# Extra rows of w4 on five DMA engines, wide value products on four column groups, and a new order of the tail

## The chip, the cores and the metric

The kernel runs on one core of one Trainium2 chip. Its engines are named PE (matmul; PEld is its weight load), DVE (vector), ACT (scalar), POOL (GpSimd) and SP, which here only issues DMAs. The metric is the device time in microseconds of one execution; the median over several is used. The profile's span runs from the first to the last instruction of the program, so an execution's time is somewhat longer than its span.

## The reference

One token (B = S = 1, D = 512) passes a layer norm; an attention over the last 4096 of 32768 cached positions, with 32 heads of 128, is multiplied by a gate that comes from a small MLP, and the input is added:

```python
def reference(...):
    x = A_x
    xn = _layernorm(x)
    s = _A_ref(xn, A_k_cache, A_v_cache, A_wq, A_wo)   # attention, below
    g = _silu(_B_ref(xn, B_w1, B_w2, B_w3, B_w4))
    return x + s * g

# _A_ref, W = 4096, Dh = 128, 32 heads
q = (xn @ wq) per head
scores = einsum("bhqd,bhkd->bhqk", q, k_cache[:, :, -W:]) * Dh ** -0.5
o = einsum("bhqk,bhkd->bhqd", softmax(scores), v_cache[:, :, -W:])
return o.reshape(1, 1, 4096) @ wo

# _B_ref, S = 1: the shifts by one and two positions leave only zeros of h
x1 = xn + shifted @ w2                                  # shifted is all zeros
return x1 + _gelu(_layernorm(x1) @ w3) @ w4             # w3 512x1376, w4 1376x512
```

All inputs and the output are bf16. Keys and values of the window are 32 MB each; with the weights 78.84 MB are read from HBM.

## The kernel before, in words

Everything is loaded through SP's queue, by one helper `load` (L79), in program order: w2, w3, w4, wq, then keys and values. A transfer that needs a buffer which is still in use holds up SP, and all transfers behind it.

**Start.** x is normalised; the MLP runs as a chain of small steps on PE, ACT, DVE and POOL: `a_ps` (L217, the product with w3, whose columns are split into ten chunks of 128 and one of 96), gelu into `a_bf`, `hr_ps` (L225, L228: rows of w2 and w4 as moving operand, 512 wide, one matmul for each chunk), the gate `g_row`. Then q: `qT_ps` (L244) and its broadcast `q_bc`. The tiles of tag "misc" share one PSUM buffer, so each of these steps waits for the one before it to be read out. Outside the region described next, a scheduler places the instructions on their engines.

**Groups.** The 32 heads are taken in 8 groups of 4 (`G`). A group's keys are one 4 MB transfer (`load_kv`), its values another. A tile `kv` has 128 partitions and `CP` = 128 columns of 128 elements. The keys' scores are formed in two ways: columns 0 to `nd(g)` - 1 (64 to 80) on DVE (`k_vector`: product L308, sum L310, four parts), the others on PE (`k_turn`: transposes L324, copied out by ACT L326; `k_scores` L332). The softmax of a group is cut into `sm_own`, `sm_max`, `sm_turn` (L354, L356, L358), `sm_exp` (L363 to L370), `sm_den` (L376) and `sm_rden` (L381).

**Values.** `v_part` multiplies the values by the probabilities `pT`. Ordinary groups use 128 matmuls with a weight load of 128x128 values and 4 moving columns (L430). The groups in `MOVED` use 32 matmuls that load 16 columns of `pT` and move four columns of values, 512 wide (L422), into `ov`; ACT copies it (L425), and `v_add` (L437), in the next step, adds the four wanted blocks. `v_out` scales by the softmax's denominator into `o_blk`.

**Order.** In `tc.manual_schedule` the program's order on PE, DVE and ACT is the order written. Step s handles the keys of group s and the values of group h = s - 2. There are three buffers for keys (one of them is later used for a part of wo) and two for values, so the values of group 7 can be loaded only when those of group 5 have been used, which is the last PE work of step 7. Steps 8 and 9 are the tail: the last softmax, the values of groups 6 and 7, the latter in three pieces (`cuts`, columns 64, 112, 128).

**Output.** o times wo is taken in blocks of heads: 16 heads in a 512 wide product (`y_wide`), 8 (`y_block(1)`) and the last 8. A block's o is first redistributed over the partitions: `ox_spread` (DVE), `ox_pick` (a matmul L468, then DVE L470 and L474). The product is `rows_add` (L150): four matmuls of 128 columns, each with a weight of one column, into four rows 32 partitions apart of `y_ps`. Of the last 8 heads, the first 320 rows of wo (`wo_few`, two loads of 160 KB, with 5 as the outer dimension of their access pattern) go through `ox_few`, the rest head by head (`y_head`, `wo_rows`). `few` and `perm` are permutation matrices made from the identity.

The lines that the text speaks of stand below.

Of the kernel before, what the change touches and what calls it, by code (L numbers as in the profile page):

```python
# [24 lines left out]
LATE = 7  # L25
MOVED = (0, 2)


@with_exitstack
def kernel(  # L30
# [27 lines left out]
    F = B_w3.shape[1]  # L58
    assert F == 10 * P + 96
    scale = float(Dh) ** -0.5  # L60
# [28 lines left out]
    load(w3_sb[:], B_w3.rearrange("(p c) n -> p c n", p=P))  # L89
    w4_sb = wts.tile([P, 11, D], BF16, name="w4_sb")  # L90
    load(w4_sb[:, 0:10, :], B_w4[0:10 * P, :].rearrange("(p c) n -> p c n", p=P))
    load(w4_sb[0:96, 10, :], B_w4[10 * P:F, :])
    wq_sb = wts.tile([P, KC, HD], BF16, name="wq_sb")

    load(wq_sb[:].rearrange("p c n -> p (c n)"), A_wq.rearrange("(a b c) n -> b a (c n)", a=2, c=KC))

# [78 lines left out]


    x_f = small.tile([P, KC], FP32, name="x_f")
    nc.vector.tensor_copy(out=x_f[:], in_=x_bf[:])
# [6 lines left out]

    perm = wts.tile([P, P // 2, 2], BF16, name="perm")
    nc.vector.tensor_copy(out=perm[:], in_=ident_bf[:].rearrange("k (a b) -> k b a", a=2))
    xq_ps = ps_tr.tile([P, KC], FP32, tag="pt", name="xq_ps")
# [22 lines left out]

    chunks = [(P, slice(r, 10 * P, 10)) for r in range(10)]
    chunks += [(96, slice(10 * P, F, 1))]
    a_ps = ps_misc.tile([P, 11], FP32, tag="misc", name="a_ps")
    for j, (m, cols) in enumerate(chunks):
        for c in range(KC):
            nc.tensor.matmul(a_ps[0:m, j:j + 1], lhsT=w3_sb[:, c, cols], rhs=z3_bf[:, c:c + 1],  # L217
                             start=(c == 0), stop=(c == KC - 1))
    a_bf = small.tile([P, 11], BF16, name="a_bf")
    nc.scalar.activation(out=a_bf[:, 0:10], in_=a_ps[:, 0:10], func=ACT.Gelu_apprx_tanh)  # L220
    nc.scalar.activation(out=a_bf[0:96, 10:11], in_=a_ps[0:96, 10:11], func=ACT.Gelu_apprx_tanh)

    hr_ps = ps_misc.tile([1, D], FP32, tag="misc", name="hr_ps")
    for c in range(KC):
        nc.tensor.matmul(hr_ps[:], lhsT=shifted_bf[:, c:c + 1], rhs=w2_sb[:, c, :], start=(c == 0),  # L225
                         stop=False)
    for i, (m, _) in enumerate(chunks):
        nc.tensor.matmul(hr_ps[:], lhsT=a_bf[0:m, i:i + 1], rhs=w4_sb[0:m, i, :], start=False,  # L228
                         stop=(i == len(chunks) - 1))
# [30 lines left out]
    make_masks(8)  # L260

    few = const.tile([P, 2, 32], BF16, name="few")
    nc.vector.memset(few[:], 0.0)
    for c in range(2):
        nc.vector.tensor_copy(
            out=few[:, c, 0:4 * NE].rearrange("p (a b) -> p a b", b=4),
            in_=ident_bf[:, 4 * NE * c:4 * NE * (c + 1)].rearrange("p (b a) -> p a b", b=4))

# [16 lines left out]
    nc.vector.tensor_scalar(out=md[:], in0=ident_f[0:1 + G, 1:1 + G], scalar1=-1.0, scalar2=1e30,  # L289
                            op0=ALU.add, op1=ALU.mult)  # L290

    st = {}
# [91 lines left out]

    blocks = [(0, 16), (16, 8), (24, 8)]
    few_block = 2
    few_h = blocks[few_block][0]
    FEW = 8 * 8 * NE
    h_part = few_h + FEW // P

    r_part = FEW % P
    o_blk, wo_blk, ox_blk = {}, {}, {}
# [4 lines left out]

    def load_few():
        t = wo_blk[few_block]
        for c in range(2):  # L400
            r0 = few_h * P + c * FEW // 2
            load(t[32 * c:32 * c + 4 * NE],
                 A_wo[r0:r0 + FEW // 2, :].rearrange("(b a t) n -> a b (t n)", b=4, a=NE))

    def wo_row(h):
        return wo_rows[:, h - h_part, :]

    def load_rows(h, n):
        if h == h_part:
            load(wo_rows[r_part:P, 0, :], A_wo[h * P + r_part:(h + 1) * P, :])  # L410
            h, n = h + 1, n - 1
        load(wo_rows[:, h - h_part:h - h_part + n, :],
             A_wo[h * P:(h + n) * P, :].rearrange("(h p) n -> p h n", p=P))
# [3 lines left out]
    def v_part(g, v, c0=0, c1=CP):  # L417
        s = st[g]
        if g in MOVED:
            s["ov"] = ps_o.tile([4 * G, 4, Dh], FP32, tag="oT", name="ov")  # L420
            for c in range(0, CP, 4):
                nc.tensor.matmul(s["ov"][:], lhsT=s["pT"][:, c:c + 4, :].rearrange("p i a -> p (i a)"),  # L422
                                 rhs=v[:, c:c + 4, :], start=(c == 0), stop=(c == CP - 4))
            s["ov_sb"] = sm_pool.tile([4 * G, 4, Dh], FP32, tag="ov_sb", bufs=1, name="ov_sb")
            nc.scalar.copy(out=s["ov_sb"][:], in_=s["ov"][:])  # L425
            return
        if c0 == 0:
            s["oT"] = ps_o.tile([P, G], FP32, tag="oT", name="oT")
        for c in range(c0, c1):
            nc.tensor.matmul(s["oT"][:], lhsT=v[:, c, :], rhs=s["pT"][:, c, :], start=(c == 0),  # L430
                             stop=(c == CP - 1))

    def v_add(g):
        s = st[g]
        s["oT"] = ps_misc.tile([P, G], FP32, tag="misc", name="oT")
        for j in range(4):
            nc.tensor.matmul(s["oT"][:], lhsT=s["ov_sb"][:, j, :], rhs=ident_f[0:4 * G, G * j:G * j + G],  # L437
                             start=(j == 0), stop=(j == 3))

    def v_out(g):  # L440
        h = G * g
        b = [i for i, (h0, _) in enumerate(blocks) if h >= h0][-1]
        if b not in o_blk:
            o_blk[b] = sm_pool.tile([P, blocks[b][1]], BF16, tag=f"o{b}", bufs=1, name="o")
            if b == few_block:
                nc.gpsimd.memset(o_blk[b][:], 0.0)
        c = h - blocks[b][0]
        if g >= NG - 2:
            nc.vector.tensor_tensor(out=o_blk[b][:, c:c + G], in0=st[g]["oT"][:], in1=st[g]["rden"][:],  # L449
                                    op=ALU.mult)  # L450
            return
        for k in range(G):
            nc.scalar.mul(o_blk[b][:, c + k:c + k + 1], st[g]["oT"][:, k:k + 1], st[g]["rden"][:, k:k + 1])  # L453
# [23 lines left out]

    def ox_few(i):
        of_ps = ps_misc.tile([64, 8], FP32, tag="misc", name="of_ps")
        nc.tensor.matmul(of_ps[:], lhsT=few[:].rearrange("p a b -> p (a b)"), rhs=ox_blk[i][:],  # L480
                         start=True, stop=True)
        of = sm_pool.tile([64, 8], BF16, tag="of", bufs=1, name="of")
        nc.vector.tensor_copy(out=of[:], in_=of_ps[:])
        ox_blk[i] = of


    y_row = small.tile([1, D], FP32, name="y_row")
# [13 lines left out]
    def y_block(i):  # L501
        for t in range(8):
            rows_add(y_ps, ox_blk[i][:, t:t + 1], wo_blk[i][:, t, :], False)

    def y_head(h):
        rows_add(y_ps, o_blk[few_block][:, h - few_h:h - few_h + 1], wo_row(h), h == H - 1)

# [6 lines left out]
    for s in range(NG + LAG):  # L514
# [3 lines left out]
        if s == LAG:  # L518
            wts_guard.__exit__(None, None, None)
            v_pool = ctx.enter_context(tc.tile_pool(name="v", bufs=V_BUFS))  # L520
            wo_blk[few_block] = v_pool.tile([64, 8, D], BF16, tag="wo_few", bufs=1, name="wo_few")
            nc.gpsimd.memset(wo_blk[few_block][:], 0.0)
            wo_rows = v_pool.tile([P, H - h_part, D], BF16, tag="wo_rows", bufs=1, name="wo_rows")
            nc.gpsimd.memset(wo_rows[0:r_part, 0, :], 0.0)
        if last:
            load_rows(h_part, 2)
            v = load_kv(v_pool, A_v_cache, h, cuts)
            for r, n in ((H - G, 2), (H - 2, 1), (H - 1, 1)):
                load_rows(r, n)
        elif h >= 0:  # L530
            v = load_kv(v_pool, A_v_cache, h)
# [4 lines left out]
        if h == 5:  # L536
            load_wo(1)
            load_few()

# [40 lines left out]
        elif s == NG:  # L580

            sm_den(NG - 2)
            sm_rden(NG - 2)
            sm_turn(NG - 1)
            ox_spread(1)
            sm_exp(NG - 1)
            ox_pick(1)
            y_block(1)
            rows_add(y_ps, one_f, y_row, False)
            v_part(h, v)  # L590
            v_out(h)
            ox_spread(few_block)
            sm_den(NG - 1)
            sm_rden(NG - 1)
            ox_pick(few_block)
            ox_few(few_block)
        else:
            v_part(h, v, 0, cuts[1])
            y_block(few_block)
            for r in range(h_part, H - G):  # L600
                y_head(r)
            for c0, c1 in zip(cuts[1:], cuts[2:]):
                v_part(h, v, c0, c1)
            v_out(h)
            for r in range(H - G, H):
                y_head(r)
# [36 lines left out]
```

## Time and profile before

| what | value |
| --- | --- |
| times of four runs | 194.95, 195.37, 195.49, 196.83 us; median 195.43 |
| the profiled execution | 195.49 us, span 193.6 us |
| instructions | 4769, of them PE 2123 matmuls with as many weight loads |
| PE, PEld, DVE, ACT, POOL busy | 136.2, 103.0, 143.7, 87.2, 6.4 us |
| HBM read | 78.84 MB, 407 GB/s over the span |
| mean granted TensorE clock | 0.667 of full |

Busy time of an engine counts only instructions that compute. A row of the timeline gives start and length in us, engine, line, operation, what it writes and reads, shapes, how many were joined, and in brackets how long the engine stood idle before and what released it; "issue" means that the profile shows nothing it waited for. A row of the chain gives start, length, and what the time went to. The rows of digits cut the span into 40 slices of 4.84 us.

### The profile page before, as it was taken

To read this page: it belongs to the slowest core of one execution; us is meant where nothing else is said; L and a number is where in the kernel's file an instruction comes from. 1 tells how busy PE (TensorE), PEld (TensorE's weight loads), DVE (VectorE), ACT (ScalarE), POOL (GpSimd) and SP (SyncE) were. 2 spreads that over 40 slices of the span, in tenths; PEclk is the share of its full clock that TensorE was granted. 3 is DMA by queue.
4 is the path that set the end of the run, shared out by engine and by line. 5 is a ranking of instruction groups with operands and counts; after the bars stand their busy time and mean duration, and the time that the engine had idled before them with its cause. 6 is when DMAs were issued, how large, how long until landed. Compare 5 with 4: busy or idle time off the path is not lost.

```text
span 193.6 us, 4769 instructions
## 1 busy us (share of the span) xinstructions
PE 136.2 (70%) x2123; PEld 103.0 (53%) x2123; DVE 143.7 (74%) x162; ACT 87.2 (45%) x195; POOL 6.4 (3%) x14
## 2 busy tenths in 40 slices
PE   0559774987726589888898978820978968835782
PEld 0454363866625533567784348720868357824761
DVE  1550108999999999999999999980999999931201
ACT  2003003888896350498567056810574088723000
POOL 2110008000000000000000000000000000000000
PEclk9999955575765557996555798555555696755555
DMA  5999899999999999999999999999999999999970
GB/s 202 424 498 433 372 416 425 406 433 430 433 430 433 433 435 430 433 433 430 433 430 433 430 433 416 450 430 430 433 433 425 433 430 405 459 431 371 417 294 1
DMA packets 4725, 79.13 MB, mean 409 GB/s; under 512 B 666, under 2 KB 1466, under 8 KB 1722
## 3 DMA queue, kind: packets, MB, share of 16 engines
q1 hardware_dynamic: 4554, 78.84, 95.7%
q8 instruction: 16, 0.26, 0.5%
q10 hardware_dynamic: 152, 0.00, 0.0%
q14 instruction: 3, 0.02, 0.0%
HBM read 78.84 MB, written 0.00 MB: 407 GB/s over the span
## 4 chain that ended last, share of the span: by engine, by line
DVE 43%; DMA 31%; PE 18%; issue 4%; ACT 3%; POOL 1%; POOLq 0%; ACTq 0%; SPq 0%
DVE S L310 25%; DMA kv<-in_A_v_cache_dram 15%; DMA kv<-in_A_k_cache_dram 14%; DVE prod L308 14%; PE oT L430 6%; DMA x_bf<-in_A_x_dram 2%; PE hr_ps L228 2%; PE pt L324 2%; PE qT_ps L244 2%; ACT kt L326 2%; PE a_ps L217 1%; PE y_ps L150 1%; PE hr_ps L225 1%; PE sT L332 1%; DVE S L346 1%
## 5 line engine op out<-in xcount | busy, mean ns | idle before, releaser
L310 DVE TENSOR_REDUCE S<-prod 128x20 f32<-128x2560 bf16 (+2 forms) x32 | 82.2, 2570 | 1.1
L326 ACT COPY kt<-pt 128x1024 bf16<-128x1024 bf16 (+1 forms) x56 | 54.7, 1008 | 21.3 <-PE pt L324 20.6
L324 PE MATMUL pt<-ident_bf,kv 128*128 128x128 bf16 x444 | 46.5, 274 | 8.5 <-DMA kv<-in_A_k_cache_dram 8.5
L308 DVE TENSOR_TENSOR prod<-kv,q_bc 128x2560 bf16<-128x2560 bf16 (+2 forms) x32 | 43.5, 1361 | 8.0 <-DMA kv<-in_A_k_cache_dram 5.6
L324 PEld LDWEIGHTS <-kv 128*128 128x128 bf16 x444 | 37.5, 126 | 10.5 <-DMA kv<-in_A_k_cache_dram 8.9
L332 PE MATMUL sT<-qT_bf,kt 128*128 128x4 bf16 x444 | 20.7, 168 | 17.1 <-ACT kt L326 16.2
L332 PEld LDWEIGHTS <-kt 128*128 128x128 bf16 x444 | 17.1, 104 | 24.6 <-ACT kt L326 24.2
L430 PE MATMUL oT<-pT,kv 128*128 128x4 bf16 x768 | 22.1, 166 | 6.8 <-issue 5.4
L430 PEld LDWEIGHTS <-kv 128*128 128x128 bf16 x768 | 21.4, 104 | 8.8 <-issue 6.1
L422 PE MATMUL ov<-kv,pT 128*16 128x512 bf16 x64 | 19.9, 486 | 0.0
L370 ACT ACTIVATE pT<-S,mb 128x128 bf16<-128x128 f32 x32 | 13.9, 570 | 0.3
L422 PEld LDWEIGHTS <-pT 128*16 128x16 bf16 x64 | 6.8, 109 | 12.1 <-issue 8.0
L449 DVE TENSOR_TENSOR o<-oT,rden 128x4 bf16<-128x4 f32 x2 | 0.3, 162 | 12.7 <-PE oT L430 12.7
L453 ACT ACTIVATE o<-oT,rden 128x1 bf16<-128x1 f32 x24 | 4.3, 260 | 11.8 <-PE oT L430 9.2
L341 ACT ACTIVATE own<-sT,par 128x48 f32<-128x48 f32 (+2 forms) x32 | 7.6, 361 | 3.7 <-PE sT L332 3.7
L425 ACT COPY ov_sb<-ov 16x512 f32<-16x512 f32 x2 | 1.1, 575 | 15.6 <-PE ov L422 15.6
L370 ACT ACTIVATION_READ_ACCUMULATOR pT<-S,mb 128x1 f32 x32 | 8.2, 255 | 0.0
L231 DVE COPY hr<-hr_ps 1x512 f32<-1x512 f32 x1 | 0.7, 679 | 8.6 <-PE hr_ps L228 8.6
L496 PE MATMUL yr_ps<-wo,ox 128*1 128x512 bf16 x16 | 5.2, 494 | 0.9 <-DVE ox L474 0.9
L220 ACT ACTIVATE a_bf<-a_ps 128x10 bf16<-128x10 f32 x1 | 0.2, 179 | 11.9 <-PE a_ps L217 11.9
L363 PE MATMUL mb_ps<-md,par_t 5*128 5x4 f32 x16 | 4.2, 329 | 1.7 <-DVE md L358 1.0
L363 PEld LDWEIGHTS mb_ps<-md,par_t 5*128 5x128 f32 x16 | 3.6, 276 | 2.1 <-PE sT L332 1.1
(117 smaller groups left out, 90.3 us busy)
## 6 DMA issues: line engine op xcount, KB each, us to landing
kv<-in_A_k_cache_dram SPq DMA_DIRECT2D x7, 4096.0 KB, 29.7
kv<-in_A_v_cache_dram SPq DMA_DIRECT2D x7, 4096.0 KB, 33.3
wq_sb<-in_A_wq_dram SPq DMA_DIRECT2D x1, 4096.0 KB, 18.2
kv<-in_A_k_cache_dram SPq DMA_DIRECT2D x2, 2048.0 KB, 22.5
wo<-in_A_wo_dram SPq DMA_DIRECT2D x1, 2048.0 KB
kv<-in_A_v_cache_dram SPq DMA_DIRECT2D x1, 2048.0 KB, 11.5
kv<-in_A_v_cache_dram SPq DMA_DIRECT2D x1, 1536.0 KB, 14.6
w_sb<-in_B_w_dram SPq DMA_DIRECT2D x1, 1376.0 KB
```

The source lines that it names most:

```text
L308: nc.vector.tensor_tensor(out=prod[:, 0:m, :], in0=kn[:, rows, :], in1=q_bc[:, g:g + 1, :].to_broadcast([P, m, Dh]), op=ALU.mult)
L310: nc.vector.tensor_reduce(out=st[g]["S"][:, rows], in_=prod[:, 0:m, :], axis=AX.X, op=ALU.add)
L324: nc.tensor.transpose(pt[:, c - c0, :], kn[:, c, :], ident_bf[:])
L326: nc.scalar.copy(out=kts[b][:, 0:c1 - c0, :], in_=pt[:, 0:c1 - c0, :])
L332: nc.tensor.matmul(st[g]["sT"][:, c - nd(g), :], lhsT=kt[:, c - c0, :], rhs=qT_bf[:, G * g:G * g + G], start=True, stop=True)
L341: nc.scalar.mul(s["own"][:, 0:m, a], s["sT"][:, 0:m, a], par[:, a:a + 1])
L363: nc.tensor.matmul(mb_ps[:], lhsT=par_t[:].rearrange("k b a -> k (b a)"), rhs=md[:], start=True, stop=True)
L370: nc.scalar.activation(out=s["pT"][:, :, a], in_=s["S"][:], func=ACT.Exp, scale=scale, bias=mb[:, a:a + 1], accum_out=s["sum"][:, a:a + 1])
L422: nc.tensor.matmul(s["ov"][:], lhsT=s["pT"][:, c:c + 4, :].rearrange("p i a -> p (i a)"), rhs=v[:, c:c + 4, :], start=(c == 0), stop=(c == ...
L430: nc.tensor.matmul(s["oT"][:], lhsT=v[:, c, :], rhs=s["pT"][:, c, :], start=(c == 0), stop=(c == CP - 1))
L453: nc.scalar.mul(o_blk[b][:, c + k:c + k + 1], st[g]["oT"][:, k:k + 1], st[g]["rden"][:, k:k + 1])
L496: nc.tensor.matmul(yr[i][:], lhsT=ox_blk[i][:, t:t + 1], rhs=wo_blk[i][:, t, :], start=(t == 0), stop=(t == n - 1))
```

## The change

- **w4.** Its 1376 rows were 10 x 128 + 96; they are now 8 x 128, 32, and 320 rows in a tile of their own, `w4_few` (64 partitions, zeroed by POOL first), loaded by two transfers of 160 KB with 5 as the outer dimension. On PE the product with w3 has 17 chunks in place of 11 (8 of 128 columns, one of 32, 8 of 40), there are three gelus, a permutation matmul `af_ps` with its copy, and 17 matmuls with w4 in place of 11.
- **wq** is read in four blocks in place of two (same size of each contiguous piece), and `perm` follows.
- **Values.** `MOVED` holds groups 0 to 5. `ov` has 128 partitions; a matmul of zeros clears it, and matmul i goes to the 16 partitions from 32 (i mod 4). `v_add` uses `fold`, which adds the four groups.
- **wo.** The last 8 heads are two blocks of 4: `wo_4`, one load of 512 KB redistributed like the others with masks of 4, and the last four heads head by head. `wo_few`, its POOL memset, `ox_few` and the loads of rows of heads 26 and 27 are gone.
- **Tail.** In step 8 the exponentials of group 7 and the values of group 5 (`v_add`, `v_out`) come first, then block 1's redistribution, the values of group 6, and only then `y_block(1)` and the wide row. `ox_pick` of block 2 stands in step 9, after the first piece of group 7's values.

```diff
-MOVED = (0, 2)
+MOVED = (0, 1, 2, 3, 4, 5)
...
-    w4_sb = wts.tile([P, 11, D], BF16, name="w4_sb")
-    load(w4_sb[:, 0:10, :], B_w4[0:10 * P, :].rearrange("(p c) n -> p c n", p=P))
-    load(w4_sb[0:96, 10, :], B_w4[10 * P:F, :])
+    w4_sb = wts.tile([P, 9, D], BF16, name="w4_sb")
+    load(w4_sb[:, 0:8, :], B_w4[0:8 * P, :].rearrange("(p c) n -> p c n", p=P))
+    load(w4_sb[0:32, 8, :], B_w4[F - 32:F, :])
+    w4_few = wts.tile([64, 8, D], BF16, name="w4_few")
+    nc.gpsimd.memset(w4_few[:], 0.0)
+    for c in range(2):
+        f0 = 8 * P + 32 * NE * c
+        load(w4_few[32 * c:32 * c + 4 * NE],
+             B_w4[f0:f0 + 32 * NE, :].rearrange("(b a t) n -> a b (t n)", b=4, a=NE))
...
-    load(wq_sb[:].rearrange("p c n -> p (c n)"), A_wq.rearrange("(a b c) n -> b a (c n)", a=2, c=KC))
+    load(wq_sb[:].rearrange("p c n -> p (c n)"), A_wq.rearrange("(a b c) n -> b a (c n)", a=4, c=KC))
...
+    chunks = [P] * 8 + [32] + [8 * NE] * 8
...
+    af_ps = ps_misc.tile([64, 8], FP32, tag="misc", name="af_ps")
+    nc.tensor.matmul(af_ps[:], lhsT=few[0:8 * NE].rearrange("p a b -> p (a b)"), rhs=a_bf[0:8 * NE, 9:17],
+                     start=True, stop=True)
+    af_bf = small.tile([64, 8], BF16, name="af_bf")
+    nc.vector.tensor_copy(out=af_bf[:], in_=af_ps[:])
...
+    make_masks(4)
...
+    fold = const.tile([P, 32], FP32, name="fold")
+    nc.vector.tensor_reduce(out=fold[:], in_=ident_f[:].rearrange("p (q m) -> p m q", m=32), axis=AX.X,
+                            op=ALU.max)
...
-    blocks = [(0, 16), (16, 8), (24, 8)]
+    blocks = [(0, 16), (16, 8), (24, 4), (H - G, G)]
...
-            s["ov"] = ps_o.tile([4 * G, 4, Dh], FP32, tag="oT", name="ov")
-            for c in range(0, CP, 4):
-                nc.tensor.matmul(s["ov"][:], lhsT=s["pT"][:, c:c + 4, :].rearrange("p i a -> p (i a)"),
-                                 rhs=v[:, c:c + 4, :], start=(c == 0), stop=(c == CP - 4))
+            s["ov"] = ps_o.tile([P, 4, Dh], FP32, tag="oT", name="ov")
+            nc.tensor.matmul(s["ov"][:], lhsT=zero_bf[:], rhs=zero_bf[:].unsqueeze(1).to_broadcast([P, 4, Dh]),
+                             start=True, stop=False, skip_group_check=True)
+            for i in range(CP // 4):
+                c, r = 4 * i, 32 * (i % 4)
+                nc.tensor.matmul(s["ov"][r:r + 4 * G], lhsT=s["pT"][:, c:c + 4, :].rearrange("p i a -> p (i a)"),
+                                 rhs=v[:, c:c + 4, :], start=False, stop=(i >= CP // 4 - 4),
+                                 skip_group_check=True)
...
-            nc.tensor.matmul(s["oT"][:], lhsT=s["ov_sb"][:, j, :], rhs=ident_f[0:4 * G, G * j:G * j + G],
+            nc.tensor.matmul(s["oT"][:], lhsT=s["ov_sb"][:, j, :], rhs=fold[:, G * j:G * j + G],
...
-        if g >= NG - 2:
+        if g >= NG - 3:
...
-            wo_blk[few_block] = v_pool.tile([64, 8, D], BF16, tag="wo_few", bufs=1, name="wo_few")
-            nc.gpsimd.memset(wo_blk[few_block][:], 0.0)
+            wo_blk[2] = v_pool.tile([P, 4, D], BF16, tag="wo_4", bufs=1, name="wo_4")
             wo_rows = v_pool.tile([P, H - h_part, D], BF16, tag="wo_rows", bufs=1, name="wo_rows")
-            nc.gpsimd.memset(wo_rows[0:r_part, 0, :], 0.0)
         if last:
-            load_rows(h_part, 2)
...
             load_wo(1)
-            load_few()
+            load_wo(2)
...
             sm_turn(NG - 1)
+            sm_exp(NG - 1)
+            v_add(h - 1)
+            v_out(h - 1)
             ox_spread(1)
-            sm_exp(NG - 1)
             ox_pick(1)
+            v_part(h, v)
+            v_out(h)
+            ox_spread(2)
             y_block(1)
             rows_add(y_ps, one_f, y_row, False)
-            v_part(h, v)
-            v_out(h)
-            ox_spread(few_block)
             sm_den(NG - 1)
             sm_rden(NG - 1)
-            ox_pick(few_block)
-            ox_few(few_block)
         else:
             v_part(h, v, 0, cuts[1])
-            y_block(few_block)
-            for r in range(h_part, H - G):
-                y_head(r)
+            ox_pick(2)
+            y_block(2)
```

## The prediction

> **What bounds the kernel now.** I read the page first: engines, DMA slices, queues.
>
> ```profile
> DVE  1550108999999999999999999980999999931201
> ...
> DMA  5999899999999999999999999999999999999970
> GB/s 202 424 498 433 372 416 425 406 433 430 433 430 433 433 435 430 433 433 430 433 430 433 430 433 416 450 430 430 433 433 425 433 430 405 459 431 371 417 294 1
> ...
> q8 instruction: 16, 0.26, 0.5%
> ```
>
> The DMA engines are full from slice 1 to slice 37 at some 430 GB/s; 78.84 MB at 430 is 183 of the 193.6 us. DVE is nearly as full. Both bytes and rate stay, so time can move where the stream starts, where it could run dry, and in the tail. The 16 instruction transfers of 0.26 MB are 16 KB each. Next the chain, for who waits for whom.
>
> ```profile
> 108.49 27.18 DMA kv<-in_A_k_cache_dram
> ...
> 149.54 28.21 DMA kv<-in_A_v_cache_dram
> 177.75 0.05 issue
> ```
>
> The keys of group 6 were issued 27 us ahead of landing, the values of group 6 28 us ahead: engines may be late by many microseconds before the stream runs dry. Third, the waits: how long DVE stood still for keys before step 6.
>
> ```profile
> DVE prod L308 <- DMA kv<-in_A_k_cache_dram: 5.6, 1, 5.6
> ```
>
> It is one wait of 5.6 us, ending at 135.7; DVE work ahead of it may slip so far for nothing. Last, the timeline of PE in the tail.
>
> ```profile
> 177.79 2.21 PE L430 MATMUL oT<-pT,kv 128*128 128x4 bf16 x77 [1.35 <-DMA kv<-in_A_v_cache_dram]
> 180.24 1.50 PE L430 MATMUL oT<-pT,kv 128*128 128x4 bf16 x51 [0.24 <-issue]
> 181.61 0.57 PE L376 MATMUL den_ps<-sum,ones_f 128*128 128x4 f32 x2
> 182.45 0.21 PE L468 MATMUL ox_ps<-spread,to 128*128 128x64 bf16 x1 [0.28 <-DVE rden L381]
> ...
> 183.38 1.87 PE L430 MATMUL oT<-pT,kv 128*128 128x4 bf16 x64
> 185.18 0.48 PE L150 MATMUL y_ps<-wo_few,of 64*1 64x128 bf16 x9
> 186.43 0.80 PE L150 MATMUL y_ps<-wo_few,of 64*1 64x128 bf16 x23 [0.78 <-issue]
> ...
> 187.47 1.86 PE L430 MATMUL oT<-pT,kv 128*128 128x4 bf16 x64
> 189.59 0.59 PE L150 MATMUL y_ps<-wo_rows,o 128*1 128x128 bf16 x16 [0.25 <-DVE o L449]
> ```
>
> The tail starts with the values of group 6 (177.75), then takes the three pieces of group 7. Data end at 189 (the rate by windows falls to 89 GB/s in 188 to 189), and PE ends its values at 189.33. So PE's chain and the data end together: shortening one alone gains little, lengthening PE's shows in full. Two gaps here are marked "issue": PE waits for no engine. Others like them, and the rows used for prices:
>
> ```profile
> 69.20 9.95 PE L422 MATMUL ov<-kv,pT 128*16 128x512 bf16 x32
> ...
> 129.59 0.38 PE L430 MATMUL oT<-pT,kv 128*128 128x4 bf16 x9 [2.90 <-issue]
> ...
> 171.26 0.27 PE L430 MATMUL oT<-pT,kv 128*128 128x4 bf16 x4 [1.79 <-issue]
> ...
> 174.89 1.02 PE L150 MATMUL y_ps<-wo,ox 128*1 128x128 bf16 x32 [0.62 <-DVE ox L474]
> ```
>
> From the stall at 171.26 to that at 180.24, PE runs 4+2+1+2+1+32+8+77 = 127 matmuls, from there to 186.43 51+2+1+1+64+9 = 128. Each has its weight load: 256 instructions, one 16 KB transfer. I read these gaps as PE reaching instructions still under way. The DMA windows show instruction transfers starting in 168.5:169.5, 177.5:178.5 and 183.5:184.5, each before such a stall. The time from entering one block until the next is there was 9.0 us (171.26 to 180.24), 6.2 (180.24 to 186.43), 5.6 (165.6 to 171.26), 7.0 (122.6 to 129.6) and 5.9 (87.5 to 93.4), each start found by counting back 128 matmuls. The median is 6.2.
>
> The Trainium skill ("Runtime: NRT & Kernel Launch", "Instruction fetch mechanics") has the same 16 KiB blocks of 256 instructions, but calls the crossing "mostly hidden". By it the stalls would be nothing and the time 195.1; the 2.90, 1.79 and 0.78 us above speak against it here.
>
> **The start.** The 96 rows of w4 become 32 rows plus two loads of 160 KB into w4_few; total weight bytes are the same. These two loads wait for a POOL memset (the old wo_few one, same shape, took 3.50 us). From the start of POOL's work (0.9) or behind the identities (1.8) it ends at 4.4 to 5.3; the two issues (1.71 us before) and wq's (0.65) then end by 6.8 to 7.7; the first packet came 1.0 us after the first issue: 7.8 to 8.7. What is queued ahead (3.0 MB) lasts to about 9. Queued behind on SP are wq and keys 0 to 2, which flow later still. Cost 0, bound 0 to 0.5 us.
>
> PE's start chain grows. L217: 24 more matmuls, of which 44 took 2.78 us (63 ns) while the contiguous ones of L244 took 27 ns; the old ten full chunks become eight, so 0.3 to 1.5 us, taken 0.6 since most loads are narrow. af_ps and its copy: 0.4, as of_ps (183.28 to 183.64). A third gelu: 0.1. L228: 6 more at 0.37 to 0.42 (15 matmuls in 5.74): 2.5. In all 3.6 us, on the way to q and DVE's first prod at 29.48. DVE then reaches the 5.6 us wait with 2.0 left: the cover is that wait. The few-, fold- and mask-4 operations (some 1.5 us) lie in DVE's free time of 12.8 to 21.5; if they did not, the wait covers them too. Group 6's keys land up to 1.6 us later, since the five engines carry 64 KB each from the start, where an even split is 20 KB (44 KB at 27 GB/s per engine). That gives DVE more room and moves steps 6 and 7 by 1.6. wq read with a=4 in place of 2 has descriptors of the same size: 0.
>
> **Values of groups 0 to 5.** Four of them had 128 small matmuls (3.4 to 3.7 us), two had 32 wide ones (9.95, 311 ns each). Now all have 32 wide ones on four column groups and a zeroing one. Nearest row: the 32 of L150 at 174.89 go to four column groups and take 32 ns each at a granted clock of 0.50, while eight transposes of the same 128 columns took 0.61 to 1.01 (76 to 126 ns): a factor of 2.4 to 4. So 311/4 to 311/2.4 ns times 32 plus 0.31: 2.8 to 4.5 us; I take 3.2. That lies beside DVE's work and gains nothing by itself. Its use is the issue of the last values, which waits for group 5's (171.56). It moves by +1.6 (keys late), -1.8 (stall gone, as no block edge falls there by the count below), -0.4: to about 171. By the issue list 74.1 MB are queued ahead of them, so they flow from about 175 and have to be issued by 174: 3 us of cover. v_add for four more groups (8 matmuls, 1.05) and an ov_sb copy (0.58 on ACT, in place of four products at 0.26) lie in PE's and ACT's gaps; queued behind v_add are the next transposes, and DVE has its own work meanwhile.
>
> **The tail.** PE's order becomes: values of 6 (128), y_block(1) (32), y_row (8), den (2), first piece of 7 (64), ox_pick(2), y_block(2) (16), the other pieces (64), four heads (16). of_ps, 16 matmuls of y_block and 8 of heads go. But ox_pick now stands behind the first piece, with PE idle during DVE's pick and ox: 182.45 to 183.28 was 0.83; smaller tiles, 0.75.
>
> Values of 6 have 512 KB of wo ahead in place of 320: 192 KB at 430 GB/s is +0.45, less three instruction transfers (0.1): 178.1. Without a stall: 3.7, 1.02, 0.60, den 0.45 beside the rest: 183.9; the piece 1.87: 185.8; ox_pick 0.75, y_block 0.5: 187.05; 64 matmuls 1.86: 188.9, which is 0.4 under 189.33.
>
> Now the block edges. Ahead of group 6's values stood 1807 matmuls; now 1807 + 31 (start) - 380 (four times 128 to 33) + 2 (two zeroings) + 32 (v_add) - 40 (y_block(1), y_row) = 1452. The old edge at 1807 + 77 = 1884, less three times 128, is 1500: 48 matmuls into group 6's values, at 179.5. The next is 128 on, 6 into the first piece, which PE reaches at 184.1. It is there at 179.5 + 6.2 = 185.7: stall 1.6. Then 58 matmuls 1.7, ox_pick 0.75, y_block 0.5, 64 matmuls 1.86: 190.5. The edge after is 5 into the last piece, at 190.2; the last block of before came 3.4 us after its edge, so 189.1: no stall. The end follows as before, 4.27 us (189.33 to 193.6): span 194.8, +1.2. With the 1.9 us around it 196.7; the profiled execution (195.49) is 0.06 above the median, so 196.6.
>
> **Rivals.** (1) Fewer instructions in the tail and no stall: the block is there within 4.6 us of its edge: 195.49 - 0.4 = 195.1. For it: of 16 blocks most stalled nothing. Against: only runs of small matmuls use up 128 in so short a time, and this is one. If in addition the slack rates of 170 to 184 (411, 376, 409, 406 GB/s for 430, 1.0 us lost) went with the 192 rows of 1 KB, 194.1. (2) The block takes 9.0 us as it did from 171.26: 2.8 more, 199.4; at 7.0, 197.4. For it: lanes are full until 184. Against: one of five. (3) Slower: the column groups do not overlap, so each group costs 10.3 us. Step 6's values then end 6.7 late, step 7's transposes stand behind them on PE, and group 5's values end at 166.07 + 1.6 + 6.7 + 10.3 = 184.7; the last values flow at 185.7 in place of 175, +10.7: 206. It decides from 4.7 us per group (171 plus twice the excess over 3.2 reaches 174). Against it stand the 32 ns of L150, whose 32 weight loads took 0.73 us, all in one row group. For it, that only one-column weights were seen there, and 16 are loaded here. The Trainium skill ("TensorE: Matmul & The Clock Gate", Part 3) speaks for it too: weight loads overlap running matmuls only when the row group differs.
>
> **How the numbers follow.** A measurement of this kernel can tell about 1% from no change: 193.5 to 197.4. Forecast (stall of 0.7 to 2.4 us, 195.7 to 197.4): 0.45. Rival 1: 0.24 between 194.1 and 195.7, 0.05 below 193.5. Rival 2 beyond 197.4: 0.16. Rival 3: 0.06. Stream dry at the start beyond its bound: 0.04. So faster 0.05, same 0.69, slower 0.26. Range 194.5 to 198.8.
>
> **What would show it.** Right: 13 or 14 instruction transfers; L422 groups near 3 us; an "issue" gap of 1 to 2.5 us early in the first piece of group 7; values ending near 190.5. Wrong: no such gap, an L422 group above 5.4 us, a hole in the DMA slices at the start or near 176, or DVE with no wait for group 6's keys.

## The result and the profile after

The changed kernel takes 195.98 us (median of 53 runs) against 195.54 (79 runs of before); the ratio is 1.0028, 95% interval 1.0016 to 1.0041: slower by 0.3 to 0.8 us, less than a third of the 1% named as what a measurement can tell, resolved only because so many runs were made. Its profiled span is 194.1 us, before 193.6. Below, kernels are compared by the ratio to the runs of before on the same chip, which leaves disturbed runs out; medians hold them.

The page of the changed kernel: DVE, DMA and instruction transfers, and the group of DVE's products with its idle time.

```profile
DVE  1580011999999999998999999999999989941101
...
DMA  6999999999999999999999999999999999999960
GB/s 201 414 438 432 429 429 436 424 432 429 432 429 434 432 429 432 432 432 432 429 432 432 429 432 415 446 432 432 429 432 427 429 432 392 463 415 392 398 261 4
...
q8 instruction: 14, 0.23, 0.5%
...
L329 DVE TENSOR_TENSOR prod<-kv,q_bc 128x2560 bf16<-128x2560 bf16 (+2 forms) x32 | 43.5, 1359 | 1.6 <-ACT q_bc L285 1.3
```

The stream has no hole, at the start or near the end. DVE no longer waits for keys: the 5.6 us of before are used up. There are two instruction transfers fewer. The chain ends as before with the values of group 6:

```profile
153.27 24.98 DMA kv<-in_A_v_cache_dram
178.25 0.05 issue
```

From there PE's timeline is the whole story:

```profile
178.30 3.57 PE L440 MATMUL oT<-pT,kv 128*128 128x4 bf16 x128
181.80 1.02 PE L156 MATMUL y_ps<-wo,ox 128*1 128x128 bf16 x32
...
183.73 0.30 PE L440 MATMUL oT<-pT,kv 128*128 128x4 bf16 x6
184.81 1.68 PE L440 MATMUL oT<-pT,kv 128*128 128x4 bf16 x58 [0.78 <-issue]
186.35 0.17 PE L476 MATMUL ox_ps<-spread,to 128*128 128x16 bf16 x1
187.00 0.60 PE L156 MATMUL y_ps<-wo,ox 128*1 128x128 bf16 x16 [0.48 <-DVE ox L482]
187.53 1.57 PE L440 MATMUL oT<-pT,kv 128*128 128x4 bf16 x53
189.36 0.43 PE L440 MATMUL oT<-pT,kv 128*128 128x4 bf16 x11 [0.25 <-issue]
190.04 0.59 PE L156 MATMUL y_ps<-wo_rows,o 128*1 128x128 bf16 x16 [0.25 <-DVE o L457]
```

An edge is the place where PE passes from one block of 128 matmuls with their weight loads into the next. The edge counted to lie 6 matmuls into the first piece of group 7 is there: 6, a gap of 0.78 us, 58. So is the one 5 into the last piece (48 + 5 = 53, then 0.25). Values end at 189.79 in place of 189.33, +0.46, and the span is +0.5.

### The profile page after: what moved, and what is told of

It is laid out like the page before. It is cut to its first block, busy times and chain, and to the rows that moved or that the text cites. A ratio compares the mean times of both kernels' runs of the same rounds, so it can differ in the third digit from the quotient of the medians.

```text
span 194.1 us, 4089 instructions
## 1 busy us (share of the span) xinstructions
PE 138.5 (71%) x1783; PEld 100.9 (52%) x1783; DVE 145.5 (75%) x168; ACT 89.8 (46%) x196; POOL 5.9 (3%) x12
## 4 chain that ended last, share of the span: by engine, by line
DVE 50%; PE 27%; DMA 15%; issue 4%; ACT 2%; POOL 0%; POOLq 0%; ACTq 0%
DVE S L331 29%; DVE prod L329 15%; DMA kv<-in_A_v_cache_dram 13%; PE pt L345 4%; PE oT L447 4%; PE oT L440 4%; PE hr_ps L255 3%; PE a_ps L236 2%; DMA x_bf<-in_A_x_dram 2%; PE qT_ps L271 2%; PE ov L431 2%; PE y_ps L156 1%; PE sT L353 1%; ACT kt L347 1%; PE hr_ps L250 1%
## 5 line engine op out<-in xcount | busy, mean ns | idle before, releaser
L345 PE MATMUL pt<-ident_bf,kv 128*128 128x128 bf16 x444 | 49.8, 287 | 2.7 <-DMA kv<-in_A_k_cache_dram 2.7
L345 PEld LDWEIGHTS <-kv 128*128 128x128 bf16 x444 | 40.7, 133 | 7.2 <-DMA kv<-in_A_k_cache_dram 3.6
L431 PE MATMUL ov<-kv,pT 128*16 128x512 bf16 x192 | 20.7, 608 | 0.0
L447 PE MATMUL oT<-fold,ov_sb 128*128 128x4 f32 x48 | 10.3, 338 | 12.7 <-DVE rden L402 12.5
L447 PEld LDWEIGHTS oT<-fold,ov_sb 128*128 128x128 f32 x48 | 9.8, 303 | 13.2 <-DVE rden L402 12.9
L461 ACT ACTIVATE o<-oT,rden 128x1 bf16<-128x1 f32 x20 | 3.6, 264 | 19.9 <-PE oT L447 19.9
L431 PEld LDWEIGHTS <-pT 128*16 128x16 bf16 x192 | 5.8, 122 | 11.7 <-issue 11.2
L440 PEld LDWEIGHTS <-kv 128*128 128x128 bf16 x256 | 7.4, 105 | 2.3 <-issue 1.4
L440 PE MATMUL oT<-pT,kv 128*128 128x4 bf16 x256 | 7.6, 166 | 1.1 <-issue 1.0
L435 ACT COPY ov_sb<-ov 128x512 f32<-128x512 f32 x6 | 3.5, 585 | 10.4 <-PE ov L431 10.4
L375 PE MATMUL mt_ps<-ident_f,m 128*1 128x128 f32 x8 | 3.0, 372 | 4.9 <-DVE rden L402 4.4
```

The costliest lines, as they stand in the source:

```text
L345: nc.tensor.transpose(pt[:, c - c0, :], kn[:, c, :], ident_bf[:])
L431: nc.tensor.matmul(s["ov"][r:r + 4 * G], lhsT=s["pT"][:, c:c + 4, :].rearrange("p i a -> p (i a)"), rhs=v[:, c:c + 4, :], start=False, sto ...
L447: nc.tensor.matmul(s["oT"][:], lhsT=s["ov_sb"][:, j, :], rhs=fold[:, G * j:G * j + G], start=(j == 0), stop=(j == 3))
```

## The experiments

**Moving the edges.** The theory: PE runs into instructions still under way, at places fixed by a count of 128 matmuls. The rival: the gap belongs to its place (late data, a buffer). The edit adds n matmuls of zeros, 4 columns wide, where PE waits anyway; n = 64, 40 and 128:

```diff
             keys(0, 2)
+            if s == 4:
+                for _ in range(64):
+                    nc.tensor.matmul(y_ps[:, 0:4], lhsT=zero_bf[:], rhs=ident_bf[:, 0:4], start=False,
+                                     stop=False, skip_group_check=True)
```

> The changed kernel with 64 more matmuls on PE in step 4 (zeros times 4 columns, added into y_ps), in a stretch where PE waits for DVE anyway; nothing else moves. Theory (PE reaches instructions that are still under way, one block per 128 matmuls): the edge that lay 48 matmuls into the values of group 6 moves ahead of them, to the den matmuls near 173; the next lies some 112 into them, at 181.5, and its block is there by 178 to 180; the gap of 0.78 us in the first piece of group 7 and that of 0.25 in the last are gone or move, values end 0.7 to 1.0 us earlier, time 195.0 to 195.4. Rival (the gap belongs to the place: the piece's data or its buffer are late): the gap stays 6 matmuls into the first piece, time 195.9 to 196.1.

Measured 195.03 us, ratio 0.9986 (0.9967 to 1.0006). The first piece, in the timeline of this kernel, runs through:

```profile
178.36 3.58 PE L440 MATMUL oT<-pT,kv 128*128 128x4 bf16 x128 [2.29 <-DMA kv<-in_A_v_cache_dram]
183.79 1.85 PE L440 MATMUL oT<-pT,kv 128*128 128x4 bf16 x64
...
186.95 1.86 PE L440 MATMUL oT<-pT,kv 128*128 128x4 bf16 x64
189.07 0.70 PE L156 MATMUL y_ps<-wo_rows,o 128*1 128x128 bf16 x16 [0.25 <-DVE o L457]
```

More instructions, and faster than the changed kernel: the intervals of the two ratios do not meet. PE waits 2.29 us for the values of group 6, since here its work ahead was done at 176.06 in place of 178.18. Values end near 188.81. The edge has not left the tail: it lies 5 matmuls into block 2's product, whose 16 matmuls take 0.83 us here and 0.60 in the changed kernel. One thing else moved: the last values were issued at 171.46 in place of 173.02 (the granted clock was 1.0 in the last wide group, 0.50 in the changed kernel). That is not what made it faster: two kernels below issue them at 169.38 and 170.06, keep the gap in the first piece (1.12 and 1.14 us) and take 195.9 us.

> The same with 40 more matmuls. Theory of the blocks: the edge lies 8 into the values of group 6, near 178.5, the next 128 on, some 8 into the product of block 1 near 182.1, and its block is there 5.2 to 6.2 us after the first edge, 183.7 to 184.7: a gap of 1.6 to 2.6 us ahead of nearly all work that follows; values end 0.8 to 1.8 us later than in the changed kernel, time 196.5 to 197.7. Rival of the place: gap unmoved in the first piece of group 7, time 195.9 to 196.1.

Measured 197.36 us, ratio 1.0101 (1.0068 to 1.0133). The gap stands where it was counted, after 8 matmuls of block 1's product, with 24 to go; the next edge, 128 further, gives another of 0.54:

```profile
184.24 0.81 PE L156 MATMUL y_ps<-wo,ox 128*1 128x128 bf16 x24 [1.91 <-issue]
```

> The same with 128 more matmuls, a whole block, as a control. Theory of the blocks: edges at the same places as in the changed kernel, gaps 6 into the first piece of group 7 and 5 into its last, time 195.8 to 196.2. If the 64 and 40 act by their work in step 4 and not by moving edges, 128 acts more strongly than either.

Measured 197.88 us, ratio 1.0141 (1.01 to 1.0182): the edges came back (a gap of 0.78, 6 into the first piece), the time did not. Two things differed: the block of the second edge took longer (a gap of 1.53 in place of 0.25), and the added matmuls had delayed the steps after them, so that the values of group 7 were issued at 173.83 in place of 173.02.

```profile
190.67 0.43 PE L440 MATMUL oT<-pT,kv 128*128 128x4 bf16 x11 [1.53 <-issue]
```

As a control it was flawed; the same 128 were put where PE waits for the keys of group 1:

```diff
             k_open(s)
+            if s == 1:
+                for _ in range(128):
+                    ...
```

> Control once more: the changed kernel with 128 more small matmuls of zeros, this time at the start of step 1, where PE waits for the keys of group 1 until 43; in step 4 they had delayed steps 5 to 7 and the issue of the last values (173.83 for 173.02). Theory of the blocks: edges again 6 into the first piece of group 7 and 5 into its last, the last values issued by 173.1, data end 188.9 to 189.3, time 195.7 to 196.2. Rival (more instructions cost by their number): 196.8 to 198.

Measured 195.93 us, ratio 1.0033 (1.0006 to 1.006), that of the changed kernel, with the same gap in the first piece (at the second edge no gap shows):

```profile
184.75 1.69 PE L440 MATMUL oT<-pT,kv 128*128 128x4 bf16 x58 [0.79 <-issue]
```

So it is not the number of instructions that counts but where the edges fall: shown by 64 (gone from the first piece), 40 (moved as counted), 128 (back). Counted through the traces, 1628 and 1756 matmuls stand ahead of the two gaps of the changed kernel, which is the prediction's 1500 and one and two blocks; in every run each "issue" gap within the values and products of the tail stands at the same remainder by 128, which is 92.

The instruction packets in the traces also show why the same edge costs more in one kernel than in another. From an edge in the tail it took 1.5 to 3.8 us until the next 16 KB packet started, 0.9 to 1.4 for the packet, and, where PE stood waiting, 1.2 to 1.6 until it went on. The first part varies most: from the edge at 184.8 it was 1.9 us in the changed kernel, 3.6 with 128 in step 4. What makes a packet start late was not tested; from the last edge of each run, with the data at their end, it was 1.0 to 1.7.

**PE's order in the tail.**

```diff
             y_block(1)
+            ox_pick(2)
...
             v_part(h, v, 0, cuts[1])
-            ox_pick(2)
```

> The changed kernel with the redistribution of block 2 (its matmul and the two DVE operations) moved from behind the first piece of group 7 to behind the product of block 1, in step 8; number of instructions and edges unchanged. Theory that PE's order in the tail sets the end: the 0.5 us in which PE stands behind the first piece are hidden, values end 0.5 earlier, time 195.4 to 195.6. Rival (the second piece's data or the last rows of wo set the end): the second piece starts on its data instead, gain under 0.2 us, time 195.8 to 196.0.

Measured 195.96 us, ratio 1.0043 (1.0011 to 1.0076): no gain. But not for the rival's reason: no piece waits for a DMA. The gap in the first piece was longer in this execution (1.13 us in place of 0.78) and took most of the gain:

```profile
185.37 1.74 PE L440 MATMUL oT<-pT,kv 128*128 128x4 bf16 x59 [1.13 <-issue]
```

With the 64 matmuls that free the piece of its edge:

> The 64 extra matmuls that moved the edges out of the tail, and the redistribution of block 2 ahead of the first piece of group 7. Theory (PE's order sets the end once no block edge stalls it, and the gain of the second alone was eaten by the gap in front of it): the second piece starts near 186.3 in place of 186.95, values end near 188.2, time 194.5 to 194.8. Rival (data of the second piece or the last rows of wo set the end): second piece waits for a DMA, or the last heads do, time 194.9 to 195.2.

Measured 195.1 us, ratio 0.9997 (0.9966 to 1.0029): again nothing. The first piece and the new order save what was expected (block 2's product starts at 185.57 in place of 186.15), and the next edge, 5 into that product, takes it back:

```profile
183.80 1.85 PE L440 MATMUL oT<-pT,kv 128*128 128x4 bf16 x64
...
187.09 0.49 PE L156 MATMUL y_ps<-wo,ox 128*1 128x128 bf16 x11 [1.14 <-issue]
187.51 1.87 PE L440 MATMUL oT<-pT,kv 128*128 128x4 bf16 x64
```

Both expectations missed for one reason: once edges stall, PE goes at the pace of the blocks, and work moved within a block only changes the length of the gap. That the last rows of wo would bound the end soon after is possible (with 64 the heads took 0.70 us in place of 0.59) but was not isolated.

**Column groups.**

```diff
-                c, r = 4 * i, 32 * (i % 4)
+                c, r = 4 * i, 0
...
-                                 rhs=v[:, c:c + 4, :], start=False, stop=(i >= CP // 4 - 4),
+                                 rhs=v[:, c:c + 4, :], start=False, stop=(i == CP // 4 - 1),
```

> The changed kernel with all 32 wide matmuls of a group sent to the same column group (partitions 0 to 15) in place of four in turn; number and size of the instructions unchanged. Theory (four column groups run beside each other): a group takes 9.9 to 10.5 us in place of 3.6, those of steps 6 and 7 add up on PE, the last values are issued some 12 us later than the 173 of the changed kernel, the DMA engines run dry after 174, time 205 to 208. Rival (they did not overlap before either, the rows are only short by the way they are recorded): groups and time as in the changed kernel, 196.

Measured 209.39 us in two runs, ratio 1.0721 (1.0636 to 1.0807), above the 205 to 208 expected. Below are the groups of steps 6 and 7 from the timeline, the DMA slices of the page, and step 7's group in the changed kernel:

```profile
152.10 9.03 PE L431 MATMUL ov<-kv,pT 128*16 128x512 bf16 x32
...
177.31 8.38 PE L431 MATMUL ov<-kv,pT 128*16 128x512 bf16 x32
```

```profile
DMA  5999999999999999999999999999999998007960
```

```profile
169.38 3.59 PE L431 MATMUL ov<-kv,pT 128*16 128x512 bf16 x32
```

With four column groups step 7's group took 3.59 us in place of 8.38, so they do run beside each other. At the same clock the factor is larger still: the granted clock was 0.84 in the row of 8.38 and 0.50 in that of 3.59; at 1.0, in the kernel with 64, the group of step 7 took 1.90 us. With one column group all matmuls also write the same partitions of `ov`; which of the two counts was not separated. The last values were issued at 185.72 and the DMA engines stood empty in between: the price of rival 3, at the place it named.

**Wide or small.** `MOVED = (0, 2)`, `v_add` and `v_out` of group 5 only if it is wide, and 36 matmuls of zeros in step 4.

> The changed kernel with only groups 0 and 2 wide (groups 1, 3, 4, 5 with 128 small matmuls each), and 36 small matmuls of zeros in step 4: 384 matmuls more in all, three blocks, so the edges in the tail stay. Theory (wide values gain nothing by themselves, but keep a block edge out of group 5's values): an edge lies some 54 matmuls into the values of group 5, with a gap of 1 to 2 us there; the last values are issued at 173.5 to 175 and data end 0.5 to 1.5 us later, time 196.4 to 197.4. Rival (nothing depends on it): time 195.8 to 196.2. Rival (the wide form costs by itself): 195.2 to 195.6.

Measured 195.85 us, ratio 1.0025 (0.9996 to 1.0054). No gap in the values of group 5, and the last values were issued at 170.06, earlier than in the changed kernel. My theory fell: the edge ahead of it lies in the slower keys, so its block was there in time, as the intervals could have told me. The wide form of groups 1, 3, 4 and 5 neither gains nor costs a time that these runs resolve.

**The start.** w4 and its products as before, first with 31 matmuls of zeros in step 4 (edges unmoved), then with 95 in step 1 (edges as with 64):

> The changed kernel with w4 and its products as in the kernel before (ten chunks of 128 and one of 96, no loads of 160 KB, no permutation), and 31 small matmuls of zeros in step 4, so that the block edges stay where they are. Theory A (the longer start is covered): DVE starts some 4.5 us earlier and waits for the keys of group 6 instead, gaps in the tail as in the changed kernel, time 195.7 to 196.1. Rival B (the start uses up all cover, and the last values are issued late by it): step 7 ends 1 us earlier, the last values are issued by 172, time 195.2 to 195.6. Rival C (the 320 rows on five engines even out the engines' work): data end 0.5 to 1.5 us later than the 189.1 of the changed kernel, time 196.3 to 197.3.

Measured 196.8 us, ratio 1.0072 (1.004 to 1.0104). DVE starts at 30.26 in place of 33.71 and waits for keys, and step 7 ends no earlier (its maximum at 171.56, 171.29 in the changed kernel): rival B fell. Data end at 189.68 against 189.08. But the second gap was 1.35 us and the last values were issued at 173.28, so C was not separated from these. Hence:

> w4 and its products as in the kernel before, with 95 small matmuls of zeros in step 1 (31 to stand for those that w4 lost, and 64 that move the edges out of the tail). To be read against the changed kernel with 64. Theory (the five-engine rows even out the engines' work, worth some 0.5 us): no gap in the first piece, last values issued by 172, data end 189.5 to 189.8, time 195.5 to 196.0. Rival (they are worth nothing; the earlier run was slower by its late issue and its second gap): data end 188.9 to 189.2, time 194.9 to 195.3.

Measured 195.7 us, ratio 1.0037 (1.0009 to 1.0065), against 0.9986 (0.9967 to 1.0006) with the five-engine rows and the same edges. The last values were issued at 171.10, no gap in the first piece, but the values of group 6 land later and data end at 189.34:

```profile
178.75 3.58 PE L413 MATMUL oT<-pT,kv 128*128 128x4 bf16 x128 [3.21 <-DMA kv<-in_A_v_cache_dram]
```

So the 320 rows on five engines are worth some 0.4 us at the landing (178.75 for 178.36), and the longer start costs nothing that shows. In time the pair differs by 0.3 us in the spans of the profiled executions (193.5 and 193.2), 0.7 in the medians and 1.0 by the ratios; the two were run on different chips, and the added matmuls stand in step 1 here and in step 4 there. One landing is weak evidence: in the kernel before it was 177.79 in one execution and, with 100 matmuls added, 178.78. And that the rows even out the engines' work, as the expectation has it, is not what the traces show: the 16 completions of this transfer lie further apart with them, 174.39 to 178.31, than without, 175.13 to 178.71. Only the last comes sooner; why was not tested.

**wq.** Two blocks again, with its permutation (`a=2`).

> The changed kernel with wq read in two blocks as before, and its permutation. Theory (costs nothing, as predicted): time 195.7 to 196.2, edges and gaps as in the changed kernel. Rival (the four blocks made the stream quicker after wq: 372 to 425 GB/s in slices 4 to 6 before, 429 to 436 after): keys of group 6 land 1 us later, time 196.3 to 197.

Measured 195.9 us, ratio 1.0047 (1.0031 to 1.0062); the slices after wq stay at 429 and above: the four blocks are worth nothing that shows. The slower slices 4 to 6 of before came back in the two kernels with plain w4 (379 and 423 in slices 4 and 5 with 95) and so go with the five-engine rows; by slice 8 the bytes moved are the same to 0.2 us.

**The kernel before with other edges.** 100 matmuls of zeros in step 1.

> The kernel before with 100 small matmuls of zeros at the start of step 1. Theory of the blocks: the gap of 1.79 us in the values of group 5 goes (edge 23 into them, its block long there), the last values are issued by 170.3; the edges in the tail fall 105 into the values of group 6 and 5 into the first heads, gaps 0 to 0.6 us; values end 188.7 to 189.1, and as data end is 188.8 to 189.0 the last rows of wo then bound the end, time 194.9 to 195.3, 0 to 0.4 us below the kernel before. Rival (edges matter little in the kernel before, whose order hides them): 195.2 to 195.5.

Measured 194.68 us, ratio 0.9993 (0.9967 to 1.0019). The gaps of 1.79 and 0.24 us are gone, the one in the tail stands 5 into the heads, as counted (0.61 us):

```profile
187.83 0.27 PE L150 MATMUL y_ps<-wo_rows,o 128*1 128x128 bf16 x3 [0.61 <-issue]
```

Whether that gains stays open: the interval holds no change. Its profiled execution (span 194.2) had its data late, at 178.78, and is not typical.

No kernel tried is shown to beat the kernel before; the changed one with 64 matmuls cannot be told from it.

## Why the prediction was right, point by point

195.98 lies in the range, in the case that had the largest chance, at its lower edge (195.7 to 197.4), and on the side forecast. The mechanism was the one named: with the first piece free of its edge the changed kernel is no slower than the kernel before. The sizes were less good: 196.6 was forecast, and the gap of 0.78 us lies below the 1 to 2.5 named as a sign of being right. One sign of being wrong appeared: DVE had no wait for group 6's keys; the point on the start says how.

- **Landing of the values of group 6**: 178.1 predicted, 178.25.
- **Block edges**: places right to the matmul (6 and 5). The interval, from the entry into a block until the next is there, was the mis-sized term: 6.2 us as the median of earlier stretches; here 179.6 (178.30 plus 48 at 27.9 ns) to 184.81 is 5.2, and at the first such gap it was 5.1 to 5.9 in the other forms of the changed kernel, 6.2 in the kernel before with 100. Stall 0.78 for 1.6. The next interval, taken as 3.4 with no stall, was 4.6 (184.81 to 189.36), and the second edge cost 0.25. So the values' end (190.5, measured 189.79) was missed by 0.7 us: the first gap ended 0.9 earlier than forecast, the second gave 0.25 back, and `ox_pick` took 0.65 for 0.75 (186.35 to 187.00).
- **Start**: DVE's first product at 33.71, +4.2 for 3.6. L236 took 4.78 us for 68 matmuls, 70 ns each (63 before): narrow weight loads of strided columns were no cheaper than wide ones, +2.0 where 0.6 was taken (1.5 was the bound). L255 and L250 took 7.6 for 5.74, +1.9 for 2.5. DVE's work from there to group 6's keys took 1.2 us longer than before (101.8 for 100.6), which the prediction did not have and no run explains. So it reached the keys at 135.50, 0.1 after they had come: of the 2.0 us of cover counted on, nothing was left. That it cost nothing is in part luck; three other kernels with this start had 0.5 to 1.3 us left.
- **Keys of group 6 up to 1.6 us late**: wrong. PE took them up at 135.41, before at 135.71; they came at 134.33 with plain w4 and 31 matmuls, at 135.80 with 95. The landings scatter by nearly as much as the term.
- **Cover of the last issue**: taken to end at 174. Over the kernels with the new w4, issues at 169.38, 170.06, 171.46, 172.09 and 173.02 gave data ends of 188.85, 188.81, 189.03, 189.09 and 189.08; 173.20, 173.25, 173.83 gave 189.42, 189.25, 190.03. It ends near 173, where the changed kernel stands.
- **Wide groups**: 0.61 and 3.59, 4.2 us for 3.2, inside 2.8 to 4.5, at a granted clock of 0.50; at 1.0, with 64, 0.39 and 1.90. `v_add` took 1.87 at 175.60, not 1.05, which is the clock again: the same 8 matmuls took 1.05 at 159.74, where it was 1.0, and 1.87 here at 0.50. PE was free for the values of group 6 only at 178.18, 0.1 us ahead of the data.
- **wq at 0**: right. **POOL's memset**: 3.51 us, done at 4.4, wq issued at 6.19, no hole: right.

The Trainium skill's "mostly hidden" ("Runtime: NRT & Kernel Launch", "Instruction fetch mechanics") does not hold for such runs of small matmuls; the gaps of 0.78 to 1.91 us, moved as counted, are the measurement. What its page "TensorE: Matmul & The Clock Gate" (Part 3) says, that weight loads overlap running matmuls only when the row group differs, did not keep the column groups from running beside each other: 3.59 us, at the lower clock, for 8.4 to 9.0.

## What to carry to other kernels

When an engine runs many short instructions in a stretch that sets the end, count its instructions from a known gap to find where the next blocks begin: the time from one edge to the next, here 4.0 to 6.2 us for 128 matmuls with their loads wherever PE waited, is a floor under that stretch. A reordering tried there is judged only with the edges held in place (whole blocks of padding, put where the engine waits anyway), or what is measured is the shift of the edges. And a change on an engine with much cover shows nothing in the time: the long start and the wide groups moved DVE and PE by microseconds and the time by nothing that could be resolved.

## What the runs showed of the hardware that was not expected

Adding 64 useless matmuls made the changed kernel faster by some 0.8 us (ratios 1.0028 and 0.9986), 40 made it slower by 1.4 (1.0101). The time from an edge to the next block is not fixed, 4.0 to 6.2 us in the tails seen, mostly by when the instruction packet starts, so the same edges gave a second gap of 0.25 us in one kernel, of 1.53 in another with the edge in the same place, and none in a third. An even split of the bytes over the 16 DMA engines was not the quickest here: with two loads that complete on five engines (five completions each in the trace, 16 for keys and values), the last completion of the values of group 6 came 0.4 us earlier in one pair of traces and 0.2 in another, though the 16 completions then lay further apart.
